# Diagonal blocks of step 1 on two engines, and the low part of step 0 behind the diagonal of its high part

## The chip, the cores and the metric

The kernel runs on one core of a Trainium2 chip. The metric is device time in microseconds (us); the profile comes from one execution of the program, recorded by the hardware profiler. The core's engines are TensorE (PE, matmuls; PEld is its weight load), VectorE (DVE), ScalarE (ACT), GpSimd (POOL) and SyncE (SP), which issues most of the DMAs. Each engine runs its own instructions in the order in which they were written into the program, and waits on semaphores for the others.

## The reference

Three layers follow each other: a delta-rule attention, a two-matrix feed-forward layer, and a soft mixture of eight experts whose gate weights are balanced by row and column normalisation.

```python
B, H, S, D = 4, 8, 768, 48
k_n = k / (norm(k) + 1e-6)
for t in range(S):                                 # delta rule, state (B, H, D, D)
    y[:, :, t] = q_t @ state
    state = state + b_t * outer(k_t, v_t - state^T k_t)
x = y as (B*S, H*D) = (3072, 384)
x = leaky(x @ w_in, 0.01) @ w_out                  # 384 -> 2048 -> 384
P = exp(x @ w_gate - max), then 8 times: rows to sum 1, columns to sum N/E
out = sum over 8 experts e of P[:, e] * (relu(x @ w1[e]) @ w2[e])    # 384 -> 1024 -> 384
```

## The kernel before, in words

The sequence of 768 tokens is cut into six steps `t` of 128 tokens, and the attention is computed by blocks. For each step and each of the four batches `b` (all eight heads at once) `part1` normalises the keys, transposes them (`kT`), forms the Gram products and keeps, as `a`, the strictly upper part scaled by beta. `a` is split into two float16 tensors: `nh`, its high part, and `nl`, the rest `a - nh`. `nh` also gets ones on its diagonal (a select on GpSimd). The 32x32 blocks on the diagonal of `a` are copied into `a_d`, four copies for each batch, and `solve(t)` inverts all of them at once on VectorE, column by column (`ld`, `tm`, `xs`), ending with a transpose into `xt`. `part2(t, b)` copies the inverses into `u` (four copies), transposes `u` into `x`, and grows the inverse from blocks of 16 or 32 to 128 by products of `x` with `nh` and of `u` with `p1`, whose results ScalarE copies back. Then come the products with the values; `nh` and `nl` are both read in one of them (`r_ps`). The first two steps (`SMALL`) start from blocks of 16.

The helper `spread` makes the copies into `a_d` and `u`: on ScalarE, except that of step 0 every second one goes to VectorE.

The feed-forward layer of a step (`main_a(t)`) runs beside the attention of the next one. The weights `wa` come as 64-bit floats and are converted on the way: `convert` reads each third of a chunk (`raw`), makes `cva`, `cvs` and `cvp` on ScalarE, VectorE and GpSimd, and writes it to a scratch tensor. This starts behind step 0's inverse.

Nothing of this is issued directly. `Recorder` notes every operation with its engine, a cost and its dependencies, and a planner places them (`place`, `tails`, `order`). Each operation starts with a rank: the length of the work that depends on it, a bias (`AHEAD` for attention, `EARLY` for the maxima of the expert weights) and a random jolt drawn with `SEED`. In ten rounds (`ROUNDS`) the planner places the work forwards, compares the planned end with the best so far, and replaces the ranks by the distance from the end in a backwards placement. The ranks of the best round are used. `emit` then issues everything in planned order (line 560 in the profile) and fills planned gaps of TensorE with matmuls on constants (line 1205, and `stir`). The order of the last step's feed-forward layer and of the expert stage (from about 735 us on) is planned elsewhere, by the class `Plan`.

The list `late` holds the `nl` subtractions. Those of step 0 (`late[0:B]`) get an added dependency, kept by a real wait: they may not start before the second transpose of `u` into `x` (`turned[1]`). The select that writes the diagonal of `nh` comes after the subtraction that reads `nh`.

The lines that matter are the constants (line 50 and those around it), `spread` (line 672), `halves` and the lines behind it in `part1` (from line 766), and the use of `late` further down.

Of the kernel before, what the change touches and what calls it, by code (L numbers as in the profile page):

```python
# [15 lines left out]
ACTF = mybir.ActivationFunctionType  # L16
ALU = mybir.AluOpType
# [3 lines left out]
B, H, S, D = 4, 8, 768, 48  # L21
C = 128
# [24 lines left out]
SMALL = (0, 1)  # L47

STIR = (145, 20)
AHEAD, EARLY = 50.0, 60.0  # L50
ROUNDS, SEED = 10, 7
NEAR = 0.02
FILL = 0.5
SLACK = 4.0
# [512 lines left out]
def delta_moe_kernel(ctx: ExitStack, tc: tile.TileContext, k_l, v_l, q_l, beta_l, wa_in, wg, wc, out):  # L567
# [5 lines left out]
    pe, act, dve, pool, sp = (rec.engine(*x) for x in zip(("PE", "ACT", "DVE", "POOL", "SP"), engines))  # L573
# [49 lines left out]
    for i in range(RING):  # L623
# [3 lines left out]
            nh=ring_p.tile([128, H, C], F16, name=f"nh{i}"),  # L627
            nl=ring_p.tile([128, H, C], F16, name=f"nl{i}"),
# [38 lines left out]
    def bank(name):  # L667
        return free.tile(range(6 if early else 3))

    late, grams = [], []  # L670

    def spread(t, blk, out, src):
        if t == 0 and blk % 2:
            dve.tensor_copy(out=out, in_=src)
        else:
            act.activation(out=out, in_=src, func=ACTF.Copy)
# [5 lines left out]
    def load_k(t):  # L682
        kraw[t] = a1_p.tile([128, B, H, D], F32, tag="kraw", name="kraw")
        if t == 0:
            for b in range(B):
                sp.dma_start(out=kraw[t][:, b], in_=k_l[t, :, b])
        else:
            sp.dma_start(out=kraw[t], in_=k_l[t])
# [27 lines left out]
    def part1(t):  # L716
        kr = kraw.pop(t)
        n2 = a1_p.tile([128, B, H], F32, tag="n2", name="n2")
        sn = a1_p.tile([128, B, H], F32, tag="sn", name="sn")
        rn = a1_p.tile([128, B, H], F32, tag="rn", name="rn")  # L720
        for bs in ([slice(b, b + 1) for b in range(B)] if t == 0 else [slice(0, B)]):
            for b in range(bs.start, bs.stop):
                sq = ring[(t * B + b) % RING]["kn"][:, :, 0:D]
                act.activation(out=sq, in_=kr[:, b], func=ACTF.Square)
                dve.tensor_reduce(out=n2[:, b], in_=sq, axis=AX.X, op=ALU.add)
            n, s0, r = n2[:, bs], sn[:, bs], rn[:, bs]
            dve.tensor_scalar(out=n, in0=n, scalar1=2.0 ** -110, scalar2=None, op0=ALU.max)
            act.activation(out=s0, in_=n, func=ACTF.Sqrt)
            dve.reciprocal(out=r, in_=s0)
            dve.tensor_tensor(out=r, in0=r, in1=n, op=ALU.mult)  # L730
            dve.tensor_tensor(out=r, in0=r, in1=s0, op=ALU.add)
            dve.tensor_scalar(out=r, in0=r, scalar1=0.5, scalar2=1e-6, op0=ALU.mult, op1=ALU.add)
            dve.reciprocal(out=r, in_=r)

        def normalise(b):
            r = ring[(t * B + b) % RING]
            dve.tensor_tensor(out=r["kn"][:, :, 0:D], in0=kr[:, b],
                              in1=rn[:, b].unsqueeze(2).to_broadcast([128, H, D]), op=ALU.mult)
        yield
        for b in range(B):  # L740
            normalise(b)
            if b == B - 1 and t + 1 < NT:
                load_k(t + 1)
            r = ring[(t * B + b) % RING]
            kn, kT, nh, nl = r["kn"], r["kT"], r["nh"], r["nl"]
            ps = bank("kt_ps")
            for p in range(NP):
                pe.transpose(out=ps[:, p * C:(p + 1) * C],
                             in_=kn[:, 2 * p:2 * p + 2].rearrange("p a d -> p (a d)"), identity=ident)
            act.activation(out=kT, in_=ps, func=ACTF.Copy)  # L750
            yield
            a = (at_p if t == 0 and b > 1 else a1_p).tile([128, H, C], F32, tag="uc" if t == 0 and b > 1 else "a32", bufs=2)
            gps = [bank("g_ps").rearrange("p (h c) -> p h c", h=4) for _ in range(2)]
            for j in range(4):
                for g in range(2):
                    kk = kT[64 * g:64 * g + D, j, :]
                    pe.matmul(out=gps[g][:, j], lhsT=kk, rhs=kk, start=True, stop=True)
            for g in range(2):
                for j in range(4):
                    h = 2 * j + g  # L760
                    g1 = dve.scalar_tensor_tensor(out=a[:, h], in0=gps[g][:, j], scalar=beta[:, t, b, h:h + 1], in1=upper,
                                             op0=ALU.mult, op1=ALU.mult)
                    grams.append(g1)
                yield

            def halves():
                act.activation(out=nh, in_=a, func=ACTF.Copy)
                late.append(pool.tensor_tensor(out=nl, in0=a, in1=nh, op=ALU.subtract))

            if t:  # L770
                halves()
            for blk in range(4):
                o = 32 * blk
                spread(t, blk, a_d[o:o + 32, :, b * H:(b + 1) * H], a[o:o + 32, :, o:o + 32].rearrange("p h j -> p j h"))
            if not t:
                halves()
            pool.affine_select(out=nh, in_=nh, pattern=[[0, H], [-1, C]], compare_op=ALU.not_equal,
                               fill=1.0, base=0, channel_multiplier=1)
            yield

    xt_of = {}
# [32 lines left out]
    def part2(t, b):  # L814
# [21 lines left out]
        for blk in range(4):  # L836
            o = 32 * blk
            spread(t, blk, u[o:o + 32, :, o:o + 32], xt[o:o + 32, :, b * H:(b + 1) * H].rearrange("p j h -> p h j"))
# [272 lines left out]
    if True:  # L1111
# [22 lines left out]

        setup2()
        run(part1(0))
        setup3()
        act.activation(out=wg_r, in_=wg_f, func=ACTF.Copy)
        dve.tensor_tensor(out=wg_r[:, :, E:2 * E], in0=wg_f[:, :, 0:E], in1=fr(wg_r[:, :, 0:E]), op=ALU.subtract)
        run(solve(0))  # L1140
        run(part1(1))
        attention(0, 0)
        attention(0, 1)
# [25 lines left out]
        for t in range(NT - 1):  # L1169
            rec.bias = 0.0  # L1170
            for n, _ in enumerate(main_a(t)):
                rec.flush()
                if t and n % 3 == 0:
                    rec.after = rec.steps[-1]
                    rec.bias = EARLY
                    next(mx_gen, None)
                    rec.after, rec.slack, rec.bias = None, 0.0, 0.0
            rec.bias = AHEAD
            if t + 2 < NT:
                run(part1(t + 2))  # L1180
            for b in range(B):
                attention(t + 1, b)
            if t + 2 < NT:
                run(solve(t + 2))
# [23 lines left out]
        pe, act, dve, pool, sp = engines  # L1208
# [200 lines left out]
        for i in range(NF1):  # L1409
# [6 lines left out]
            if i in tasks:  # L1416
                n, t = tasks[i]
# [12 lines left out]
        for c in range(KD):  # L1430
# [11 lines left out]
            out=cmax[:, 2 * E + t5:2 * E + t5 + 1], in_=xmax[:, t5], axis=AX.X, op=ALU.max))],  # L1442
# [277 lines left out]
        for u, (e, p) in enumerate(units):  # L1720
# [18 lines left out]
            x = [Pair(e, p, i) for i in range(4)]  # L1739
# [93 lines left out]
```

## Time and profile before

| | us |
|---|---|
| median of 3 runs | 2193.38 |
| lowest and highest run | 2190.36, 2196.22 |
| profiled execution, its own time | 2193.52 |
| its span, first to last instruction | 2191.7 |
| TensorE busy | 2100.6 (96%) |
| VectorE busy | 1674.5 (76%) |
| ScalarE busy | 1399.2 (64%) |
| GpSimd busy | 605.7 (28%) |

The page also cuts the span into 40 equal slices of about 55 us. TensorE's busy share, in tenths, is 6 7 8 8 9 8 in the first six slices, 9 (90% or more) in nearly all the others. All attention work carries the line number 560, that of the planner's issue, so groups are told apart by the names of their tiles. A row of a timeline begins with start and duration; "x4" means that four instructions in a row were merged, and the duration is that of all of them. Brackets at the end tell how long the engine was idle before, and what released it.

### The profile page before, as it was taken

Reading aid. Unit: us, or ns where it says so; the run is one execution under the profiler, and the core shown is the slowest. Engines: PE = TensorE matmul, PEld = TensorE weight load, DVE = VectorE, ACT = ScalarE, POOL = GpSimd, SP = SyncE. Lnnn points to the kernel's source line nnn. Section 1 sums busy time; section 2 is a strip of 40 time slices with the busy share of each in tenths; the row PEclk is TensorE's granted clock in tenths of the full one; section 3 lists DMA queues with packets and bytes.
Section 4 is the critical chain, followed back from the end, with each engine's and each line's share of the span. In section 5 each row is a group of like instructions: output and inputs, shape, how many; then the busy total and the mean of one; then the engine's idle time right before and its main releaser. Section 6 shows DMA issues by size and latency. Waiting matters only on the chain.

```text
span 2191.7 us, 43420 instructions
## 1 busy us (share of the span) xinstructions
PE 2100.6 (96%) x17219; PEld 1577.7 (72%) x17219; DVE 1674.5 (76%) x3313; ACT 1399.2 (64%) x2621; POOL 605.7 (28%) x672
## 2 busy tenths in 40 slices
PE   6788989999999999999999999999999999999999
PEld 5676767887877766766677777777777777777776
DVE  8676777649685567886777877877877877877877
ACT  5978746654756467768666656656656656656554
POOL 3654621111120161335215115115114114213100
PEclk8899989999999999999999999999999999999999
DMA  3566655755565652343223223333333333333321
GB/s 99 162 200 200 217 181 172 237 195 198 183 213 193 217 204 99 107 152 130 102 95 127 102 105 138 116 109 138 116 109 137 116 109 137 116 107 117 110 95 52
DMA packets 123452, 312.89 MB, mean 143 GB/s; under 512 B 14960, under 2 KB 66800, under 8 KB 117104
## 3 DMA queue, kind: packets, MB, share of 16 engines
q1 hardware_dynamic: 121088, 306.18, 40.8%
q10 hardware_dynamic: 2160, 3.93, 0.5%
q8 instruction: 135, 2.21, 0.4%
q14 instruction: 69, 0.57, 0.1%
HBM read 247.84 MB, written 62.13 MB: 141 GB/s over the span
## 4 chain that ended last, share of the span: by engine, by line
PE 77%; DVE 10%; ACT 7%; issue 3%; POOL 2%; DMA 1%; SPq 0%; DVEq 0%; ACTq 0%; POOLq 0%
PE b L1487 25%; PE b L1586 19%; PE ph L1586 11%; PE ph L1487 6%; PE bg L560 5%; PE po L560 5%; PE ph L560 4%; ACT u L560 2%; DVE tm L560 2%; DVE xs L560 1%; DVE a L560 1%; ACT p L560 1%; ACT cva L560 1%; DVE gl L560 1%; PE ph L1339 1%
## 5 line engine op out<-in xcount | busy, mean ns | idle before, releaser
L1248 POOL TENSOR_TENSOR stg<-stg 128x128 f32<-128x128 f32 (+2 forms) x248 | 166.6, 689 | 804.4 <-ACT stg L1245 800.3
L1487 PEld LDWEIGHTS <-w1h 128*128 128x128 f16 x2112 | 204.8, 98 | 221.0 <-issue 1.7
L1487 PE MATMUL b<-xoh,w1h 128*128 128x512 f16 x864 | 327.5, 379 | 0.0
L1487 PE MATMUL b<-xoh,w1l 128*128 128x512 f16 x864 | 327.5, 379 | 0.0
L1487 PE MATMUL b<-xol,w1h 128*128 128x512 f16 x864 | 327.4, 379 | 0.0
L1251 DVE SCALAR_TENSOR_TENSOR acc<-b,pm,acc 128x192 f32<-128x192 f32 (+1 forms) x357 | 155.4, 448 | 92.5 <-PE b L1586 91.6
L1487 PEld LDWEIGHTS <-w1l 128*128 128x128 f16 x1056 | 103.3, 98 | 124.6
L1245 ACT ACTIVATE b<-b 128x512 f32<-128x512 f32 x144 | 84.1, 584 | 139.3 <-PE b L1487 138.1
L1251 DVE SCALAR_TENSOR_TENSOR acc<-ph,pm,acc 128x192 f32<-128x192 f32 (+1 forms) x231 | 98.0, 432 | 76.9 <-PE ph L1586 76.8
L1245 ACT ACTIVATE c<-b 128x512 f32<-128x512 f32 x192 | 113.8, 593 | 63.0 <-PE b L1487 62.0
L560 PE MATMUL ph<-x1h,w 128*128 128x512 f32 (+1 forms) x504 | 143.5, 400 | 5.3 <-ACT leak L560 5.3
L1251 DVE SCALAR_TENSOR_TENSOR c<-c,c 128x512 f32<-128x512 f32 x192 | 134.7, 719 | 5.9 <-ACT c L1245 3.6
L1248 POOL TENSOR_TENSOR w2l<-stg,w2h 128x576 f16<-128x576 f32 (+1 forms) x96 | 108.6, 1150 | 107.0 <-ACT w2h L1245 107.0
L560 PE MATMUL po<-gh,w 128*128 128x512 f32 (+1 forms) x504 | 137.5, 397 | 0.6 <-ACT gh L560 0.6
L1248 DVE TENSOR_TENSOR c<-c,c 128x512 f32<-128x512 f32 x192 | 136.0, 712 | 2.5
L1251 DVE SCALAR_TENSOR_TENSOR c<-b,v 128x512 f32<-128x512 f32 x144 | 97.5, 689 | 43.9 <-PE b L1487 43.2
L560 DVE TENSOR_TENSOR gl<-leak,gh 128x512 fp32r<-128x512 f32 (+1 forms) x84 | 59.5, 708 | 76.7 <-ACT leak L560 65.7
L560 PEld LDWEIGHTS ph<-x1h,w 128*128 128x128 f32 x504 | 90.7, 194 | 22.9 <-ACT leak L560 5.7
L560 PEld LDWEIGHTS po<-gh,w 128*128 128x128 f32 x504 | 90.0, 192 | 18.4 <-ACT gh L560 2.1
L1248 POOL TENSOR_TENSOR w1l<-stg,w1h 128x384 f16<-128x384 f32 (+1 forms) x64 | 85.9, 1348 | 33.7 <-ACT w1h L1245 33.7
L1245 ACT ACTIVATE b<-ph 128x512 f32<-128x512 f32 x144 | 84.2, 585 | 6.6 <-PE ph L1487 2.5
L560 ACT ACTIVATE gh<-ph 128x512 fp32r<-128x512 f32 (+1 forms) x84 | 48.1, 572 | 50.9 <-PE ph L560 48.2
(510 smaller groups left out, 6653.4 us busy)
## 6 DMA issues: line engine op xcount, KB each, us to landing
w<-wa_scratch SPq DMA_DIRECT2D x100, 768.0 KB, 4.8
acc_scratch<-acc SPq DMA_DIRECT2D x84, 384.0 KB, 2.6
acc<-acc_scratch SPq DMA_DIRECT2D x84, 384.0 KB, 3.5
stg<-wc SPq DMA_DIRECT2D x64, 384.0 KB, 8.7
xoh<-xo_scratch SPq DMA_DIRECT2D x21, 1152.0 KB, 5.1
xol<-xo_scratch SPq DMA_DIRECT2D x21, 1152.0 KB, 8.0
raw<-wa SPq DMA_DIRECT2D x48, 256.0 KB, 2.9
wa_scratch<-cvp SPq DMA_DIRECT2D x48, 256.0 KB, 3.1
```

What stands on the lines that cost most here:

```text
L560: o.last = fn(*args, **{k: x.real() if isinstance(x, View) else x for k, x in kw.items()})
L1245: return vec("ACT", n, lambda e: e.activation(out=out, in_=src, func=func, scale=scale), reads, writes, **kw)
L1248: return vec(eng, n, lambda e: e.tensor_tensor(out=out, in0=a, in1=b, op=fn), reads, writes, **kw)
L1251: return vec("DVE", n, lambda e: e.scalar_tensor_tensor(out=out, in0=a, scalar=scalar, in1=b, op0=f0, op1=f1), reads, writes, **kw)
L1339: ordered(pe.matmul(out=self.ps, lhsT=wt[:, c * 128:(c + 1) * 128], rhs=xx[:, c], start=m == 0 and c == 0, stop=m == 2 and c == KD - 1))
L1487: ordered(pe.matmul(out=banks[b], lhsT=w[:, a], rhs=x[:, c].rearrange("p s k -> p (s k)"), start=start, stop=i == 2 and (a, c) == terms[-1 ...
L1586: ordered(pe.matmul(out=banks[b][:, 0:HD], lhsT=xx[:, o:o + 128], rhs=wt[:, t], start=first and k == 0 and j == 0, stop=k == NK - 1 and j ...
```

## The change

Three things are changed. `spread` gives every second copy to VectorE in step 1 as well as in step 0; this holds for the copies into `a_d` and for those into `u`. For step 0 the order around `nl` is another: `nh` is copied, gets its ones on the diagonal, then `nl = a - nh` is taken (its diagonal comes out as -1, as `a` is zero there), and a second select sets the diagonal of `nl` to zero. Only step 0's subtractions are put into `late` now, which makes no difference to its use. For the other steps the order stays. The planner's constants are `AHEAD` 30 in place of 50 and `SEED` 1 in place of 7.

```diff
--- before.py
+++ after.py
@@ -47,8 +47,8 @@
 SMALL = (0, 1)
 
 STIR = (145, 20)
-AHEAD, EARLY = 50.0, 60.0
-ROUNDS, SEED = 10, 7
+AHEAD, EARLY = 30.0, 60.0
+ROUNDS, SEED = 10, 1
 NEAR = 0.02
 FILL = 0.5
 SLACK = 4.0
@@ -670,7 +670,7 @@
     late, grams = [], []
 
     def spread(t, blk, out, src):
-        if t == 0 and blk % 2:
+        if t <= 1 and blk % 2:
             dve.tensor_copy(out=out, in_=src)
         else:
             act.activation(out=out, in_=src, func=ACTF.Copy)
@@ -763,19 +763,22 @@
                     grams.append(g1)
                 yield
 
-            def halves():
+            def diagonal(x, value):
+                return pool.affine_select(out=x, in_=x, pattern=[[0, H], [-1, C]], compare_op=ALU.not_equal,
+                                          fill=value, base=0, channel_multiplier=1)
+
+            if t:
                 act.activation(out=nh, in_=a, func=ACTF.Copy)
-                late.append(pool.tensor_tensor(out=nl, in0=a, in1=nh, op=ALU.subtract))
-
-            if t:
-                halves()
+                pool.tensor_tensor(out=nl, in0=a, in1=nh, op=ALU.subtract)
             for blk in range(4):
                 o = 32 * blk
                 spread(t, blk, a_d[o:o + 32, :, b * H:(b + 1) * H], a[o:o + 32, :, o:o + 32].rearrange("p h j -> p j h"))
             if not t:
-                halves()
-            pool.affine_select(out=nh, in_=nh, pattern=[[0, H], [-1, C]], compare_op=ALU.not_equal,
-                               fill=1.0, base=0, channel_multiplier=1)
+                act.activation(out=nh, in_=a, func=ACTF.Copy)
+            diagonal(nh, 1.0)
+            if not t:
+                late.append(pool.tensor_tensor(out=nl, in0=a, in1=nh, op=ALU.subtract))
+                diagonal(nl, 0.0)
             yield
 
     xt_of = {}
```

## Rows read from the trace of the kernel before

**Rows 1.** Busy us of each engine in stretches, their instructions, granted clock, DMA share, GB/s.

```profile
core 0: us, PE busy (x) PEld busy (x) DVE busy (x) ACT busy (x) POOL busy (x), PEclk, DMA share, GB/s
...
0.00:45.00 45.00, 36.18 (x289) 27.93 (x289) 39.68 (x141) 25.43 (x46) 12.53 (x26) 0.89 0.35 108
45.00:53.50 8.50, 0.03 (x1) 0.03 (x2) 8.50 (x24) 3.87 (x8) 6.08 (x4) 0.80 0.09 25
53.50:110.00 56.50, 43.33 (x511) 36.14 (x512) 37.89 (x87) 51.76 (x127) 35.65 (x38) 0.88 0.52 163
110.00:200.00 90.00, 75.62 (x739) 62.73 (x739) 62.62 (x170) 71.28 (x171) 47.13 (x57) 0.92 0.62 199
200.00:310.00 110.00, 91.98 (x746) 74.23 (x745) 82.08 (x197) 80.94 (x177) 55.88 (x57) 0.97 0.63 205
310.00:735.00 425.00, 412.26 (x3317) 337.21 (x3318) 287.78 (x651) 249.60 (x472) 62.18 (x65) 0.99 0.59 198
```

**Rows 2.** Waits, 40 to 110 us: engine, line, releaser, us in total, times, longest.

```profile
PE po L560 <- POOL nh L560: 8.6, 1, 8.6
```

**Rows 3.** Timeline of TensorE: last stir matmuls, first products with nh and nl.

```profile
42.95 1.92 PE L560 MATMUL ph<-stir 128*128 128x256 f16 x16
...
53.47 0.61 PE L560 MATMUL po<-x,nh 128*128 128x64 f16 x8 [8.60 <-POOL nh L560]
...
78.56 0.21 PE L560 MATMUL bg<-uc,nl 128*128 128x48 f16 x1
```

**Rows 4.** Timeline of VectorE, 30 to 77 us.

```profile
30.32 0.64 DVE L560 TENSOR_SCALAR n<-n 128x32 f32<-128x32 f32 x1
...
32.24 0.17 DVE L560 TENSOR_SCALAR rn<-rn 128x32 f32<-128x32 f32 x1
...
44.57 2.37 DVE L560 STREAM_TRANSPOSE x<-u 128x1024 f16<-128x1024 f16 x2
...
58.53 0.29 DVE L560 TENSOR_SCALAR cvs<-cva 128x256 f16<-128x256 f32 x1 [0.38 <-ACT cva L560]
...
74.77 1.88 DVE L560 TENSOR_SCALAR cvs<-cva 128x256 f16<-128x256 f32 x1 [4.32 <-ACT cva L560]
```

**Rows 5.** Timeline of ScalarE: step 0's last nh copy, and its idle time before 50.33.

```profile
29.77 1.04 ACT L560 ACTIVATE nh<-uc 128x1024 f16<-128x1024 f32 x1
...
50.33 1.31 ACT L560 ACTIVATE a_d<-a 32x256 f16<-32x256 f32 x2 [4.57 <-DVE a L560]
```

**Rows 6.** Timeline of GpSimd, 28 to 77 us.

```profile
28.50 2.44 POOL L560 TENSOR_SCALAR_AFFINE_SELECT mt<-mt 128x512 f32<-128x512 f32 x4 [3.35 <-ACT mt L560]
42.35 1.22 POOL L560 MEMSET xs<- 128x1056 f32 x2 [11.42 <-DVE tm L560]
45.90 4.25 POOL L560 TENSOR_TENSOR nl<-a,nh 128x1024 f16<-128x1024 f32 x2 [2.32 <-DVE x L560]
51.59 0.79 POOL L560 TENSOR_TENSOR cva<-cva,cvs 128x256 f32<-128x256 f32 x1 [1.44 <-DVE cva L560]
52.33 1.09 POOL L560 TENSOR_SCALAR_AFFINE_SELECT nh<-nh 128x1024 f16<-128x1024 f16 x1
...
72.28 4.22 POOL L560 TENSOR_TENSOR nl<-a,nh 128x1024 f16<-128x1024 f32 x2
```

**Rows 7.** Copies and selects by tile: ns min/median/max, first and last start us, forms.

```profile
L560 ACT ACTIVATE a_d<-a x16: 627/648/659, 50.3 to 90.5; 32x256 f16<-32x256 f32 x16
...
L560 ACT ACTIVATE u<-tm x16: 633/658/700, 141.5 to 200.1; 32x256 f16<-32x256 f32 x16
...
L560 DVE CAST u<-tm x8: 361/380/1146, 42.3 to 90.9; 32x256 f16<-32x256 f32 x8
...
L560 DVE CAST a_d<-uc x4: 370/375/379, 16.7 to 26.0; 32x256 f16<-32x256 f32 x4
L560 DVE CAST a_d<-a x4: 374/378/574, 19.4 to 26.4; 32x256 f16<-32x256 f32 x4
...
L560 POOL TENSOR_SCALAR_AFFINE_SELECT nh<-nh x24: 1086/1092/1527, 52.3 to 627.0; 128x1024 f16<-128x1024 f16 x24
```

**Rows 8.** The stretch with TensorE's most idle time after 320 us, columns as in rows 1.

```profile
540.00:560.00 20.00, 17.32 (x87) 14.08 (x87) 16.02 (x40) 10.93 (x20) 1.14 (x2) 0.91 0.54 188
```

## The prediction

> **What bounds the kernel now.** I read the windows by stage first [rows 1]. From 310 us on TensorE is busy for 412.3 of 425 us up to 735 us; the page's 40 slices show it nearly full from there to the end. Time can be won there only by removing matmuls, and the change removes none. Ahead of 310 us nothing is full: TensorE 0.03 of 8.5 us, then 43.3 of 56.5, 75.6 of 90 and 92.0 of 110, a part of that being filler matmuls on constants. ScalarE is the fullest engine right behind the gap: 51.8 of 56.5 us (92%) from 53.5 to 110, then 79% and 74%. VectorE has 67% and 70% from 53.5 to 200, but 39.7 of 45 us (88%) in the first stage, where the norms, the Gram products and step 0's inverse run on it one after the other.
>
> The second view is the list of waits, 40 to 110 us. Its one large wait of TensorE is 8.6 us for GpSimd's nh [rows 2]. The timelines say what it is. TensorE ends its stir matmuls at 44.87 and starts the first product with nh at 53.47 [rows 3]. VectorE delivers x for batches 0 and 1 in two transposes from 44.57 to 46.94 [rows 4], so that product lacks only nh. nh itself was copied early: the last of step 0's four copies starts at 29.77 [rows 5]. GpSimd then does, in its queue, the two nl subtractions (45.90, held behind the second transpose; 4.25 us), a weight product, and only then the diagonal of nh (52.33, 1.09 us) [rows 6]. The diagonal can't go first, because the subtraction must read nh before its diagonal is overwritten. So 7.6 us, from about 45.85 to 53.47, is waiting for an order that the values don't require. ScalarE has nothing to do for 4.57 us of it [rows 5].
>
> **The change part by part.** The profiled execution took 2193.52 us (span 2191.7), 0.1 us above the median of the three runs, so sums are made against 2193.5.
>
> Step 0's low part. nh gets its diagonal straight after its copy, and nl is taken afterwards, with a second select that clears its diagonal. No DMA is moved and no queue of SP. The first nh product no longer waits for the subtraction. Late next are x (45.8) and then ScalarE, which must copy each product out. What TensorE gains is at most the 7.6 us. What the path gains is what ScalarE can do ahead of time, as ScalarE is 92% busy behind the gap: its idle 4.57 us. Ends 0 and 7.6; I take 4.6, by that row.
>
> What this costs: the four selects of 1.09 us [rows 7] go from behind the transposes to somewhere between the copies and 45.8 us. There VectorE runs step 0's inverse. A TENSOR_SCALAR on VectorE at 30.32 took 0.64 us and ended with GpSimd's selects on mt (28.50 to 30.94), where its like at 32.24 took 0.17 [rows 4, 6]: GpSimd's selects can hold up VectorE. If all four stand in the way of the inverse the cost is 4 x 1.09 = 4.4 us, if they fit beside its transposes and reductions it is nothing. No row places them; I take half, 2.2.
>
> The four new selects on nl (4 x 1.09 = 4.4 us of GpSimd) come behind the subtractions. The first reader of nl is the product at 78.56 us [rows 3], while batch 0's and 1's nl were done at 50.15 [rows 6]: 28 us of room, and GpSimd is busy for 35.7 of 56.5 us there [rows 1]. I take nothing; without that cover it is 4.4 us. The subtractions are still held behind the second transpose; what queues behind them on GpSimd is weight conversion, as now.
>
> Step 1's copies. Eight of sixteen copies into a_d go from ScalarE (0.648 us) to VectorE, and eight of sixteen into u (0.658 us) [rows 7]. The first eight lie in the 92% stretch: 8 x 0.648 = 5.2 us. Ends 0 and 5.2; at 92% I take 4.8. The second eight lie from 141 to 200 us, where ScalarE is 79% busy and VectorE also has long chains: 8 x 0.658 = 5.3 us, ends 0 and 5.3; I take half, 2.6. VectorE takes 0.38 us for such a copy [rows 7], 16 x 0.38 = 6.1 us into stretches with about 19 and 27 us idle. I cost that at nothing, covered by that idle time; without it, 6.1 us.
>
> A copy on VectorE can also be held up by GpSimd. One of the copies to u took 1.146 us, in the stretch where GpSimd filled xs (42.35, 1.22 us); one of those to a_d took 0.574 [rows 6, 7]. Over the sixteen copies that VectorE has now that is (1.146 - 0.38) + (0.574 - 0.378), about 1 us. I take 1.0 for the new sixteen; the ends are 0 and 16 x 0.77 = 12.3.
>
> The same is seen on weight conversion: a TENSOR_SCALAR on cvs took 1.88 us while GpSimd subtracted (72.28 to 76.50), against 0.29 at 58.53 [rows 4, 6]. The Trainium skill speaks against the move here (SBUF — State Buffer, Who interferes with whom): VectorE's copies, casts and tensor_scalar may use a pair of ports that GpSimd uses too, and whichever of the two comes second is blocked until the other's instruction ends. By that rule each copy that meets GpSimd would be blocked, and the sum would be that of the third rival below; these rows agree in kind.
>
> The new order. SEED and AHEAD enter only the ranks from which the planner starts; the later of its ten passes replace them, and the pass that it thinks shortest is kept. So both edits draw another order for everything up to 735 us, of a like kind. Behind 735 us the order is written by another planner that the diff doesn't touch. I take 0. The ends: a gain can't exceed the 12.7 us that TensorE idles from 310 to 735 [rows 1]; for a loss the row is the worst 20 us of that stage, 540 to 560, with 2.7 us idle [rows 8]. One more such stretch in each of the four steps is 10.7 us.
>
> **The sum.** -4.6 + 2.2 - 4.8 - 2.6 + 1.0 = -8.8; 2193.5 - 8.8 = 2184.7 us. It carries to the end because TensorE is the bound from 310 us on: its work there starts that much earlier.
>
> **The rivals.**
> The gain is eaten ahead of 310 us (0.24). ScalarE is at 79% and 74% from 110 to 310, so other chains (weight conversion through three engines, step 2's inverse) may set the pace and take up whatever arrives early. Then the copies bring nothing, and of the first part 4.6 - 2.2 = 2.4 us is left: 2191.1. For it: no engine is full there [rows 1]. Against: ScalarE is the fullest up to 110 us, and nearly as full as TensorE with its fillers up to 200.
>
> The stall stays under another name (0.08). If the planner puts the diagonals late, or batch 0's product queues behind other work, the first part gives nothing: -4.8 - 2.6 + 1.0 = -6.4, 2187.1. That would be the change not doing what it says.
>
> The port takes it back (0.06). Every new copy meets GpSimd at the 0.77 us of the one above (12.3 us), and all four selects lie on the inverse (4.4): -4.6 - 4.8 - 2.6 + 4.4 + 12.3 = +4.7, 2198.2. It turns slower once copies and selects together cost over 12.0 us. Of the sixteen copies of now only two were held up, hence the small chance. It is the rule that the Trainium skill's page SBUF — State Buffer (Who interferes with whom) states, applied to every copy.
>
> The new order is worse (0.14). TensorE is at 97% from 310 to 735, so another draw has more to lose than to win. At four stretches like 540 to 560 (+10.7), and with the head's gain down to 3.6 us, it is +7.1: 2200.6. It turns slower once the new order loses more TensorE time from 310 on than the head gives. For it: the ranks are drawn anew. Against: it is made by the same planner, which keeps its best of ten.
>
> **How the numbers follow.** Forecast 0.48; the rivals 0.24, 0.08, 0.06, 0.14. A measurement here can tell about 0.3% from no change, 6.6 us: under 2186.8 is faster, over 2200.0 slower. Faster: most of the forecast (0.44), nearly half of the stall that stays (0.04), some of the eaten gain with a lucky order (0.05) and a little more, 0.55. Slower: the worse order and the port, and lower chances within the others, 0.18, counting that the order's loss may be well above its row. Same: 0.27. The low end takes the first part at its 7.6 us, all copies (10.5) and no costs, with 2 us from the order: 2193.5 - 20.1, about 2173. The high end reaches to the port's case and most of the worse order, 2199.
>
> **What would show it.** In the changed kernel: the wait of TensorE for GpSimd's nh gone and the first product on nh near 46 us; step 0's four selects on nh ahead of 46 us, and step 0's inverse no longer than before; eight casts more on VectorE to a_d and eight more to u, near 0.38 us each; ScalarE's busy time lower by about 10 us up to 200 us; the last filler matmuls and the stretch of full TensorE some 9 us earlier; idle TensorE time from there to the end of the attention stage near 12.7 us. The prediction is wrong if step 0's inverse is longer by over 4 us, if the full stretch doesn't start earlier, or if TensorE's idle time behind it grows by more than what was won.

## The result: slower, 2212.64 us

| | before | after |
|---|---|---|
| median, us | 2194.8 | 2212.64 |
| lowest and highest run, us | 2190.36, 2196.97 | 2210.28, 2214.42 |
| span of the profiled execution, us | 2191.7 | 2212.6 |
| TensorE busy in it, us | 2100.6 | 2113.0 |

The ratio of the times is 1.0086, with a 95% interval of 1.0072 to 1.0101: 16 to 22 us slower. The forecast was 2184.7 us, its range ended at 2199, and slower had a chance of 0.18. The forecast was wrong in sign.

The windows by stage of the changed kernel answer to [rows 1] (busy us and instructions of TensorE, its weight loads, VectorE, ScalarE, GpSimd; granted clock of TensorE, DMA share, GB/s). The granted clock has two levels in these traces, full speed (2.4 GHz) and half of it (1.2 GHz); the row gives the mean over the stretch, with full speed as 1:

```profile
0.00:45.00 45.00, 31.33 (x249) 24.19 (x250) 39.47 (x137) 23.45 (x42) 16.48 (x29) 0.92 0.33 108
45.00:53.50 8.50, 4.98 (x43) 3.57 (x43) 7.05 (x8) 6.44 (x20) 4.83 (x4) 0.61 0.00 1
53.50:110.00 56.50, 44.54 (x522) 38.15 (x521) 44.80 (x101) 43.60 (x105) 30.68 (x31) 0.83 0.43 133
110.00:200.00 90.00, 75.54 (x732) 65.52 (x732) 73.77 (x176) 67.75 (x162) 45.90 (x53) 0.88 0.54 163
200.00:310.00 110.00, 87.89 (x713) 69.13 (x713) 88.60 (x212) 74.01 (x173) 55.67 (x67) 0.94 0.64 204
310.00:735.00 425.00, 403.81 (x3118) 329.91 (x3118) 278.13 (x636) 244.20 (x456) 69.89 (x65) 0.99 0.61 202
```

And the first row of its page, the busy time of the whole span:

```profile
PE 2113.0 (95%) x17252; PEld 1589.4 (72%) x17252; DVE 1696.2 (77%) x3329; ACT 1389.4 (63%) x2605; POOL 612.3 (28%) x676
```

TensorE's busy time that still lies ahead at a given moment is the page's total less the windows up to there. At 735 us it was 2100.6 - 659.4 = 1441.2 us before and is 2113.0 - 648.1 = 1464.9 us now: the changed kernel is 23.7 us behind. At 310 us it was 1853.5 and is 1868.7: 15.2 us behind. So some 15 us are lost ahead of 310 us and another 8.5 from 310 to 735, where TensorE idles 425 - 403.8 = 21.2 us in place of 12.7; behind 735 us, 2.8 us less idling comes back. The stretch ahead of 310 has two losses in these rows, and a third in the filler matmuls. TensorE idles 3.0 us more from 53.5 us on, and its granted clock is 0.83, 0.88 and 0.94 where it was 0.88, 0.92 and 0.97 [rows 1]. The mean from 53.5 to 310 us is 0.89 against 0.93; 0.04 x 256.5 is about 10 us of full-speed time, some 8 of it while TensorE was busy (208.0 us there), by this estimate. The planner's fillers (line 1205, now 1208) took 38.2 instead of 34.4 us up to 310. The whole span agrees: of the 20.9 us that it grew, 8.5 are idle time and 12.4 busy time (2.9 of filler matmuls, the rest the same products for longer).

The timelines of the changed kernel (start, duration, engine, what; in brackets the idle time before and its releaser), which answer to [rows 3 to 6]:

```profile
48.02 0.58 PE L560 MATMUL bg<-x,nh 128*128 128x64 f16 x8 [5.54 <-DVE x L560]
```

```profile
44.39 2.30 DVE L560 CAST u<-tm 32x256 f16<-32x256 f32 x4
46.72 2.37 DVE L560 STREAM_TRANSPOSE x<-u 128x1024 f16<-128x1024 f16 x2
...
51.61 1.98 DVE L560 TENSOR_SCALAR cva<-cva 128x256 f32<-128x256 f32 x1 [0.15 <-ACT cva L560]
```

```profile
48.70 1.10 ACT L560 ACTIVATE p<-bg 32x128 f16<-32x128 f32 x4 [1.77 <-PE bg L560]
```

```profile
23.69 2.28 POOL L560 TENSOR_SCALAR_AFFINE_SELECT nh<-nh 128x1024 f16<-128x1024 f16 x2
...
29.02 2.13 POOL L560 TENSOR_SCALAR_AFFINE_SELECT nh<-nh 128x1024 f16<-128x1024 f16 x2 [0.21 <-ACT nh L560]
...
49.18 2.13 POOL L560 TENSOR_TENSOR nl<-uc,nh 128x1024 f16<-128x1024 f32 x1 [3.55 <-DVE x L560]
51.27 2.17 POOL L560 TENSOR_TENSOR nl<-a,nh 128x1024 f16<-128x1024 f32 x1
```

The order is the one that was meant. nh has its diagonal by 31.15 us, ahead of the transposes; nl is taken behind them; the first product with nh starts at 48.02 instead of 53.47 us [rows 3] and waits for x, not for GpSimd; ScalarE copies its result at 48.70, where the kernel before made its first such copy at 56.70:

```profile
56.70 0.27 ACT L560 ACTIVATE p<-po 32x128 f16<-32x128 f32 x1
```

By tile (ns min/median/max, first and last start), answering to [rows 7]:

```profile
L560 DVE CAST a_d<-a x12: 362/374/1277, 19.3 to 110.6; 32x256 f16<-32x256 f32 x12
```

```profile
L560 DVE CAST u<-tm x16: 362/380/1149, 44.4 to 201.6; 32x256 f16<-32x256 f32 x16
```

```profile
L560 POOL TENSOR_SCALAR_AFFINE_SELECT nl<-nl x4: 1090/1143/1274, 63.9 to 101.9; 128x1024 f16<-128x1024 f16 x4
```

The new casts and selects cost about what was expected in the median (0.374, 0.380 and 1.143 us). What is late is something else. SP's DMA issues of converted weights, first and last, in the kernel before and then in the changed one (in the changed one the first row holds two issues):

```profile
55.26 0.60 SPq L560 DMA_DIRECT2D wa_scratch<-cvp  x1
...
266.12 0.52 SPq L560 DMA_DIRECT2D wa_scratch<-cvp  x1
```

```profile
62.07 1.26 SPq L560 DMA_DIRECT2D wa_scratch<-cvp  x2
...
298.95 0.52 SPq L560 DMA_DIRECT2D wa_scratch<-cvp  x1
```

Conversion begins 6.8 us later and ends 32.8 us later. And of TensorE's waits from 53 to 310 us in the changed kernel (us in total, times, longest) the first, now the longest, is absent from the kernel before:

```profile
PE ph L560 <- DMA w<-wa_scratch: 8.7, 5, 4.2
PE bg L1208 <- ACT p L560: 5.9, 4, 2.7
PE po L560 <- DVE gl L560: 5.9, 5, 2.6
```

### The profile page after: what moved, and what is told of

The parts are those of the page before. It is cut to its first block, busy times and chain, and to the rows that moved or that the text cites. A ratio compares the mean times of both kernels' runs of the same rounds, so it can differ in the third digit from the quotient of the medians.

```text
span 2212.6 us, 43523 instructions
## 1 busy us (share of the span) xinstructions
PE 2113.0 (95%) x17252; PEld 1589.4 (72%) x17252; DVE 1696.2 (77%) x3329; ACT 1389.4 (63%) x2605; POOL 612.3 (28%) x676
## 4 chain that ended last, share of the span: by engine, by line
PE 75%; DVE 12%; ACT 7%; issue 3%; DMA 2%; POOL 2%; SPq 0%; ACTq 0%; DVEq 0%; POOLq 0%
PE b L1490 25%; PE b L1589 19%; PE ph L1589 10%; PE ph L1490 6%; PE bg L560 5%; PE po L560 4%; PE ph L560 4%; DVE tm L560 2%; DVE xs L560 2%; ACT u L560 1%; DVE cva L560 1%; ACT a_d L560 1%; DVE gl L560 1%; DMA w<-wa_scratch 1%; DVE stir L560 1%
## 5 line engine op out<-in xcount | busy, mean ns | idle before, releaser
L560 ACT ACTIVATE gh<-ph 128x512 fp32r<-128x512 f32 (+1 forms) x84 | 48.2, 574 | 83.1 <-PE ph L560 82.0
```

The lines of the kernel that those rows point to most:

```text
L560: o.last = fn(*args, **{k: x.real() if isinstance(x, View) else x for k, x in kw.items()})
```

## The experiments

Two kinds of kernels are told apart. Those whose label begins with f keep the old planned order, instruction by instruction, and only exchange or add the instructions in question. Those that begin with c, n or s let the planner order everything anew. Those that begin with a start from the changed kernel and keep its order. The table gives the time against runs of the kernel before on the same chip, the start of VectorE's casts of step 0's inverse into u, the start of the first product with nh, and the start of the last issue of converted weights (the last three in us from the start of the span).

| kernel | ratio, 95% interval | us against before | inverse done | first nh product | last converted |
|---|---|---|---|---|---|
| before | | | 42.3 | 53.5 | 266 |
| after | 1.0086 [1.0072, 1.0101] | +18.9 | 44.4 | 48.0 | 299 |
| f_copies | 1.0019 [1.0010, 1.0028] | +4.2 | 42.4 | 54.2 | 269 |
| f_order | 1.0015 [1.0005, 1.0025] | +3.3 | 44.6 | 48.6 | 270 |
| f_both | 1.0021 [1.0011, 1.0031] | +4.6 | 44.5 | 48.1 | 270 |
| f_extra | 1.0005 [0.9995, 1.0015] | +1.1 | 42.3 | 53.4 | 266 |
| c_const | 0.9989 [0.9977, 1.0001] | -2.4 | 41.6 | 48.5 | 277 |
| c_copies | 0.9990 [0.9980, 0.9999] | -2.2 | 42.8 | 53.9 | 269 |
| c_order | 1.0095 [1.0077, 1.0114] | +20.8 | 47.3 | 50.8 | 295 |
| c_order4 | 1.0075 [1.0058, 1.0092] | +16.5 | 46.5 | 50.0 | 287 |
| c_edits | 1.0052 [1.0034, 1.0070] | +11.4 | 47.9 | 51.5 | 284 |
| n_early | 1.0007 [0.9995, 1.0020] | +1.5 | 46.1 | 49.6 | 277 |
| n_late | 0.9971 [0.9958, 0.9985] | -6.4 | 41.9 | 46.6 | 262 |
| n_extra | 1.0110 [1.0094, 1.0126] | +24.1 | 43.5 | 54.7 | 294 |
| n_extra3 | 1.0034 [1.0021, 1.0047] | +7.5 | 44.5 | 51.5 | 287 |
| s_order | 1.0052 [1.0037, 1.0067] | +11.4 | 44.8 | 48.2 | 278 |
| s_before | 1.0029 [1.0021, 1.0038] | +6.4 | 41.3 | 48.2 | 275 |
| s_copies | 1.0058 [1.0044, 1.0071] | +12.7 | 42.2 | 49.2 | 272 |
| a_act | 1.0111 [1.0091, 1.0130] | +24.3 | 44.4 | 48.1 | 307 |
| a_free | 1.0065 [1.0050, 1.0080] | +14.3 | 44.4 | 48.0 | 292 |

### Each edit in the old order

f_copies issues step 1's sixteen copies on VectorE at the places that they had on ScalarE.

```diff
+        elif t == 1 and blk % 2:
+            rec.note("ACT", nc.vector.tensor_copy, "activation", (), dict(out=out, in_=src))
```

> The order of the kernel before is kept as it was; only step 1's sixteen copies (8 into a_d, 8 into u) are issued on VectorE in their old places. Theory P (GpSimd and VectorE hold each other up, and weight conversion pays): the copies cost VectorE more than 0.38 us each and ScalarE, which runs in its old order, wins little: 0 to +6 us against before. The prediction's sum: ScalarE was the fullest engine, so -4 to -8 us. Theory D (only the new draw of the order is to blame): -2 to -8 us, since the edit itself is then a gain.

+4.2 us. ScalarE's busy time from 53.5 to 110 us falls from 51.76 [rows 1] to 46.06 us, and no time is won; the granted clock of that stretch is 0.77.

```profile
53.50:110.00 56.50, 45.77 (x484) 38.20 (x485) 40.81 (x97) 46.06 (x116) 36.77 (x39) 0.77 0.53 166
```

f_order moves step 0's selects on nh right behind the copies of nh, and puts the selects on nl in the places that they leave.

```diff
-                act.activation(out=nh, in_=a, func=ACTF.Copy)
+                o = act.activation(out=nh, in_=a, func=ACTF.Copy)
+                if not t:
+                    o.calls.append((nc.gpsimd.affine_select, (), diagonal(nh, 1.0)))
...
+            if not t:
+                o.calls[:] = [(nc.gpsimd.affine_select, (), diagonal(nl, 0.0))]
```

> The order of the kernel before is kept; only step 0's four selects on nh are issued right behind the copies of nh, and the four selects on nl take their old places. The prediction's sum: the first product with nh 6 to 7 us earlier and the end 2 to 5 us earlier. Theory C (the wait for nh never was on the chain that sets the end, since ScalarE in its own order only reaches the copies of that product at 56.7 us): the first product some 6 us earlier and the end within 2 us of before. Theory P: VectorE's inverse of step 0 up to 4 us longer, the end 0 to +4 us.

+3.3 us, though the wait for nh is gone. In f_order, TensorE's longest wait from 40 to 110 us, then the timelines of TensorE, ScalarE and VectorE:

```profile
PE bg L560 <- ACT p L560: 10.7, 1, 10.7
```

```profile
48.64 0.40 PE L560 MATMUL po<-x,nh 128*128 128x64 f16 x8
...
61.46 0.59 PE L560 MATMUL bg<-u,p 128*128 128x64 f16 x8 [10.68 <-ACT p L560]
```

```profile
52.59 1.31 ACT L560 ACTIVATE a_d<-a 32x256 f16<-32x256 f32 x2 [4.57 <-DVE a L560]
...
58.95 0.27 ACT L560 ACTIVATE p<-po 32x128 f16<-32x128 f32 x1
```

```profile
44.57 2.22 DVE L560 CAST u<-tm 32x256 f16<-32x256 f32 x4
```

The first product with nh starts at 48.64 us, and the product that takes up its result (through ScalarE's copy p) at 61.46, behind a wait of 10.68 us for that copy. ScalarE copies p at 58.95, because in its queue p stands behind the copies into a_d and nh of step 1, and these wait for VectorE's a. Its idle time ahead of them is 4.57 us, as it was [rows 5], only 2.26 us later, by as much as the inverse is later (44.57 against 42.33).

f_both joins the two edits in the old order.

```diff
+        elif t == 1 and blk % 2:
...
+                    o.calls.append((nc.gpsimd.affine_select, (), diagonal(nh, 1.0)))
```

> Both edits in the old order of the kernel before. The sum of the two runs above: the prediction's sum says -6 to -11 us, theory P 0 to +8 us, theory D -4 to -11 us. If it isn't slower than before by over 6 us, most of the 18 us that the change lost comes from the new order and not from what the edits cost by themselves.

+4.6 us; the wait is again one for p (11.2 us). In the old order the two edits of the work together cost a quarter of what the change cost when planned anew.

### The constants and each edit, planned anew

c_const takes only the constants:

```diff
-AHEAD, EARLY = 50.0, 60.0
-ROUNDS, SEED = 10, 7
+AHEAD, EARLY = 30.0, 60.0
+ROUNDS, SEED = 10, 1
```

> The kernel before with AHEAD 30 and SEED 1 and none of the other edits, planned anew. Theory D: most of the loss is here, +10 to +20 us. Theory P: the operations are those of before, so within 6 us of before, and weight conversion ends near 266 us as before, not near 298.

-2.4 us: with unchanged work, the new start of the planner (this one draw) isn't what costs 19 us.

c_copies, c_order and c_edits keep AHEAD 50 and SEED 7 and take the copies (the first of these two edits), the order of step 0's low part (the second, as in the change), or both.

```diff
-        if t == 0 and blk % 2:
+        if t <= 1 and blk % 2:
```

```diff
+            diagonal(nh, 1.0)
+            if not t:
+                late.append(pool.tensor_tensor(out=nl, in0=a, in1=nh, op=ALU.subtract))
+                diagonal(nl, 0.0)
```

> Step 1's copies alone, planned anew with AHEAD 50 and SEED 7. In the old order they cost +4 us. Theory R (the planner has to place more work on the pair VectorE and GpSimd, finds a longer order, and the loss is both): +3 to +8 us against before. Theory D (chance of one draw): anything between -6 and +8, not tied to when weight conversion ends.

> Step 0's low part alone, planned anew with AHEAD 50 and SEED 7. In the old order it cost +3 us. Theory R: the four selects on nh ahead of the inverse and the four on nl are the larger part of what the planner must place on the pair, so most of the loss is here: +8 to +15 us, and weight conversion ends well behind 266 us. The prediction's sum for this part: -2.4 us.

> Both edits, with the constants of before (AHEAD 50, SEED 7). Theory R: slower than before whatever the start, +6 to +14 us, a few us better than the changed kernel. Theory D: back near before, -6 to +3 us, since the draw alone was bad.

Copies -2.2, order +20.8, both +11.4 us. In these plans the loss comes with the edit of step 0's low part.

a_act keeps the changed kernel's order and gives step 1's copies back to ScalarE.

```diff
+            o = dve.tensor_copy(out=out, in_=src)
+            if t:
+                o.calls[:] = [(nc.scalar.activation, (), dict(out=out, in_=src, func=ACTF.Copy))]
```

> The changed kernel in its own order, with step 1's sixteen copies issued on ScalarE in their places. Theory P (the copies hold up weight conversion on VectorE and GpSimd): 4 to 10 us faster than the changed kernel, +8 to +14 us against before. If the order itself is the loss: within 4 us of the changed kernel, +14 to +22 us against before.

+24.3 against +18.9 us: in that order the copies on VectorE save some 5 us (the two numbers are known to within some 4 and 3 us). What they do depends on the order around them: they cost 4.2 us in the old order, go with a gain of 2.2 in a new plan, and save about 5 in the changed kernel's.

### Which part of the new order

n_early is c_order without the selects on nl (its diagonal keeps its -1: the step is left out); n_late also holds the selects on nh behind the second transpose, as the kernel before has them in effect. n_extra is the kernel before with the added selects on nl and nothing moved. The edits in this order, n_late's on top of n_early's:

```diff
-                diagonal(nl, 0.0)
```

```diff
+        for o, x in zip(ones_of[0:B], (turned[1], turned[1], turned[1], turned[1])):
+            o.deps.add(x)
+            o.held.add(x)
```

```diff
+            if not t:
+                pool.affine_select(out=nl, in_=nl, pattern=[[0, H], [-1, C]], compare_op=ALU.not_equal,
+                                   fill=0.0, base=0, channel_multiplier=1)
```

> Step 0's low part in the new order, but without the four selects that clear the diagonal of nl (left out, so nl keeps -1 there), planned anew with AHEAD 50 and SEED 7. If the four selects on nh ahead of step 0's inverse are the loss: +10 to +18 us, nearly that of the part with both (+20), the inverse some 2 to 5 us longer. If the four added selects are the loss: -2 to +4 us.

> As the run above (nl's diagonal not cleared, left out), but the four selects on nh of step 0 also wait for the second transpose of u into x, where the subtractions start. Only the sequence of select and subtraction differs from the kernel before. If the place ahead of the inverse is the loss: back at before, -4 to +3 us, the first copy of the inverse on VectorE near 42.3 us and the last converted weight near 266 us. If the flipped sequence itself loses (attention gets ready earlier and takes the engines from weight conversion): +6 us and more.

> The kernel before with four further selects on nl of step 0 behind those on nh (they write zeros where nl is zero already), planned anew with AHEAD 50 and SEED 7. If GpSimd's time in this stage is paid for in full, since VectorE is held up by it and weight conversion runs through both: 4.4 us of selects cost +3 to +8 us. If GpSimd has room there, as the prediction said: -3 to +3 us.

Step 0's inverse and first product with nh, in n_early:

```profile
46.09 2.19 DVE L560 CAST u<-tm 32x256 f16<-32x256 f32 x4
```

```profile
49.60 0.59 PE L560 MATMUL po<-x,nh 128*128 128x64 f16 x8 [5.33 <-DVE x L560]
```

and in n_late:

```profile
41.91 2.20 DVE L560 CAST u<-tm 32x256 f16<-32x256 f32 x4
```

```profile
46.60 0.61 PE L560 MATMUL po<-x,nh 128*128 128x64 f16 x8 [6.22 <-POOL nh L560]
```

n_early is within the noise of before (+1.5), n_late is faster (-6.4), though TensorE waits 6.22 us for nh in it. With the selects on nh beside it the inverse ends at 46.1 us, with the selects held behind it at 41.9. n_extra differs from the kernel before by four selects that change no value, and loses 24.1 us: the added selects, not the order of nh, go with the loss.

### The selects themselves, or the plan around them

f_extra adds the same four selects in the old order; n_extra3 repeats n_extra with SEED 3, c_order4 repeats c_order with SEED 4; s_order is c_order with SEED 3 and without one rule of the planner's model, by which a select on GpSimd may not run at the same time as a VectorE copy, TENSOR_SCALAR or instruction on two inputs from SBUF (for the other GpSimd operations the rule stays). The edits of f_extra and of s_order:

```diff
+            if not t:
+                o.calls.append((nc.gpsimd.affine_select, (), dict(
+                    out=nl, in_=nl, pattern=[[0, H], [-1, C]], compare_op=ALU.not_equal,
+                    fill=0.0, base=0, channel_multiplier=1)))
```

```diff
-            return lat - 0.03, lat, True
+            return lat - 0.03, lat, method != "affine_select"
```

> The kernel before in its old planned order, with one harmless select on nl issued right behind each of step 0's four selects on nh (4 x 1.09 us more on GpSimd, nothing else moved, no planning anew). Theory A (the selects cost so much only because the planner writes another order around them): 0 to +4.4 us over before, about 2195, and the last write of converted weights within 3 us of before's 266. Theory B (the selects themselves hold up the chain of weight conversion and VectorE on the chip): +12 us or more, over 2205, last write from 280 on.

> The same added selects on nl as in n_extra, planned anew from another random draw (SEED 3 in place of 7, AHEAD 50). Theory A1 (n_extra's 24 us are one bad draw): within 8 us of before, under 2201. Theory A2 (the selects push the planner to a later weight conversion whatever the draw): 2205 or more, last write of converted weights from 285 on.

> The new order of step 0's low part alone, as in c_order, planned from another draw (SEED 4 in place of 7, AHEAD 50). Theory A1 (draw): under 2201. Theory A2 (whatever the draw): 2205 or more, last write of converted weights from 285 on.

> The new order of step 0's low part alone, but the planner doesn't reserve VectorE and GpSimd against each other for a select (for subtractions and products it still does); AHEAD 50, SEED 3. Theory A3 (the reservation is what delays the conversion): last write of converted weights under 275 and the time at or under before's, 2185 to 2195. Theory A2 with real blocking on the chip: VectorE's instructions beside the selects get longer instead, and the time stays at 2203 or more.

Two of f_extra's selects on GpSimd's timeline, each on nl right behind its one on nh, and its window from 53.5 to 310 us:

```profile
52.30 1.08 POOL L560 TENSOR_SCALAR_AFFINE_SELECT nh<-nh 128x1024 f16<-128x1024 f16 x1
53.35 1.08 POOL L560 TENSOR_SCALAR_AFFINE_SELECT nl<-nl 128x1024 f16<-128x1024 f16 x1
```

```profile
53.50:310.00 256.50, 214.66 (x1993) 176.98 (x1993) 183.32 (x451) 203.79 (x473) 142.15 (x156) 0.91 0.60 193
```

The same window of the kernel before, of n_extra, and of the changed kernel:

```profile
53.50:310.00 256.50, 210.93 (x1993) 173.09 (x1993) 182.59 (x451) 203.97 (x474) 138.66 (x152) 0.93 0.60 194
```

```profile
53.50:310.00 256.50, 210.37 (x1884) 169.38 (x1884) 182.84 (x436) 200.35 (x463) 143.34 (x158) 0.87 0.54 174
```

```profile
53.50:310.00 256.50, 207.97 (x1963) 172.80 (x1962) 207.17 (x487) 185.37 (x438) 132.25 (x150) 0.89 0.56 174
```

In the old order the four selects cost 1.1 us (interval -1.1 to +3.3), with 142.15 against 138.66 us of GpSimd and the other engines' busy time hardly changed but TensorE's, whose clock is 0.91. With the same work planned anew, TensorE gets a clock of 0.87 and executes 1884 instead of 1993 matmuls, fillers among them, from 53.5 to 310 us. So the selects cost next to nothing where the order is kept, and 24.1 and 7.5 us in the two orders that the planner wrote around them.

s_before and s_copies take the same planner's rule away with no added select, from SEED 1 and, with step 1's copies on VectorE, from SEED 2. Both have s_order's edit above; s_copies also has this one:

```diff
-        if t == 0 and blk % 2:
+        if t <= 1 and blk % 2:
```

> The kernel before planned anew without reserving VectorE and GpSimd against each other for a select (subtractions and products still reserve); AHEAD 50, SEED 1. If the reservation costs real time: under 2188, TensorE further ahead at 310 us. If the chip blocks the pair just as the reservation assumed: 2190 to 2200, with longer VectorE instructions beside the selects. If a plan from another draw is all there is to it: anything within 6 us of before's 2193.

> Step 1's copies shared with VectorE, step 0's low part as before, and no reservation for selects in the plan; AHEAD 50, SEED 2. Copies worth 2 us as in c_copies and the reservation real: 2183 to 2188, faster than both kernels. If only the draw counts: 2188 to 2200, like c_copies' 2191.1 or worse.

+6.4 and +12.7 us. Without the rule, all three plans are slower than the kernel before, with the added selects (s_order, +11.4) and without: taking the rule away doesn't take the loss away. Each of the three has a draw of its own, so how much of their loss is the missing rule isn't shown.

### The wait for converted weights

a_free keeps the changed kernel's order, but step 0's feed-forward layer loads one and the same chunk each time, which is ready early.

```diff
+        if items_a[i][0] == 0:
+            o.calls[0][2]["in_"] = wa[0]
```

> The changed kernel in its own order, but in step 0 each load of converted weights takes the first chunk again, so that TensorE waits for the conversion of one chunk alone (left out: step 0 multiplies by the weights of its own chunks). If weight conversion is what paces the stage to 310 us in the changed kernel: 8 to 16 us faster than it, +2 to +10 us against before, TensorE's waits for w gone. If conversion is beside the path: within 3 us of the changed kernel.

+14.3 against +18.9 us. The two intervals (11 to 18 and 16 to 22 us) overlap, so the gain of some 5 us is hardly clear of the noise. TensorE's wait for weights falls from 8.7 to 5.5 us and doesn't vanish:

```profile
PE ph L560 <- DMA w<-wa_scratch: 5.5, 3, 3.2
```

The edit doesn't take conversion off the path. SP issues its DMAs in the written order, and the loads of w still stand behind loads and writes of the conversion, which wait for VectorE and GpSimd. In a_free, SP's longest wait in total from 225 to 262 us, and its issues ahead of the longest of TensorE's three waits:

```profile
SPq L560 <- DVE cva L560: 18.8, 8, 4.9
```

```profile
253.32 1.19 SPq L560 DMA_DIRECT2D wa_scratch<-cvp  x2
256.24 0.33 SPq L560 DMA_DIRECT2D raw<-wa  x1
256.62 0.42 SPq L560 DMA_DIRECT2D w<-wa_scratch  x1
```

So a late conversion is probably a part of the loss; how large a part stays open. It isn't all that can go wrong: s_copies has conversion done at 272 us, c_const at 277, and the first loses 12.7 us where the second loses nothing.

## Why the prediction was wrong

**The step that failed is the term of the new order: "So both edits draw another order for everything up to 735 us, of a like kind", taken at 0.** The forecast was 8.8 us faster. f_both, with the edits in the old order, is 4.6 us slower, and the changed kernel 18.9: some 13 us of the error lie in the terms for the edits themselves, and some 14 us in the order. c_const shows that the constants alone, in this draw, are harmless, as the step said. But the work had changed as well. With the planner's rule in force, six plans have the added selects (after, c_order, c_order4, c_edits, n_extra, n_extra3), and all six are slower, by 7.5 to 24.1 us. The four new plans without them (c_const, c_copies, n_early, n_late) lie between -6.4 and +1.5. The selects' own time is not it (f_extra). The rival "the new order is worse", at a chance of 0.14, named the right place, the order, but blamed the fresh draw of the ranks, which does no harm in c_const. It was also priced in the wrong stretch: by TensorE's idle time from 310 us on, at most 10.7 us (8.5 measured), while some 15 us are lost ahead of 310 us, where the rows showed no full engine and a granted clock of 0.88 to 0.97.

**"I take nothing" for the four selects on nl: right in the old order, wrong in the plan.** The 28 us of room belonged to the order of before. In the changed kernel the selects run from 63.9 us on, and the first product with nl comes at 66.85 us in place of 78.56 [rows 3]. TensorE's list of waits has none for nl there; the price shows only in the plan.

**"What the path gains is what ScalarE can do ahead of time": wrong, -4.6 us taken, none found.** The wait went, as forecast. But ScalarE's idle time of 4.57 us had VectorE's a as its releaser [rows 5], not a product of TensorE; f_order shows it unchanged, and TensorE waits for p instead. The row that was taken as the size of the gain named another cause in its brackets. In the changed kernel, where the planner moved ScalarE's work too, p is copied 8.0 us earlier (48.70 against 56.70), and TensorE is behind at 310 us all the same. The table has the same in another form: the first nh product starts anywhere from 46.6 to 54.7 us, and the time doesn't follow it (48.0 us with +18.9, 53.4 with +1.1).

**The cost of the selects beside the inverse: right in size, partly by luck.** 2.2 us were taken as half of an upper end, with no row that placed the selects. The inverse ended 2.06 us later in the changed kernel and 2.24 in f_order, but 5.0 and 5.6 us later in the plans of c_order and c_edits, above the upper end of 4.4.

**The copies: -4.8 and -2.6 us taken, +4.2 us in the old order and -2.2 planned anew.** The durations were right (0.374 and 0.380 us). What the sixteen new copies lost to GpSimd was 2.1 us in the changed kernel and 1.1 in f_copies (the sum of their times above 0.376 us each), where 1.0 was taken: the third rival, in which every copy meets GpSimd for 12.3 us in all, didn't come. ScalarE's busy time up to 200 us fell by 11.1 us (152.3 to 141.2), as forecast. That ScalarE was 92% busy didn't make it the bound: f_copies frees 5.7 us of it and gains nothing. That the copies bring nothing was the first rival, and f_order, where the wait turned up under the name of ScalarE's p, is the second.

**"The stretch of full TensorE some 9 us earlier": wrong.** TensorE is 15.2 us behind at 310 us, and idles 21.2 us from there to 735 us where 12.7 were expected. Two of the three signs of being wrong came true, this stretch and the idle time behind it; the third, an inverse longer by over 4 us, didn't.

What stays open is why the planner writes a worse order around the selects. The rows show what the worse orders have in common (a mean clock of 0.87 to 0.92 from 53.5 to 310 us, where the plans without the selects have 0.92 to 0.96; weights converted by 284 to 299 us, where those have 262 to 277), not which decision begins it. Neither sign is enough: the three plans without the rule have a clock of 0.93 to 0.95 and are done by 272 to 278 us, and still lose 6.4 to 12.7 us, two of them with no added select. That four more selects need a worse order isn't shown either: six plans were tried, no more, and the ends that the planner itself foresaw for its plans weren't compared. Of the kernels with all of the computation only c_copies has an interval below that of no change, and by a hair: 0.9990 [0.9980, 0.9999]. An order like that of n_late, with nl's diagonal cleared without GpSimd, wasn't tried.

## What to carry to other kernels

Where a program writes the order, time an edit twice, in the old order and planned anew: here the selects cost 1.1 us in the one and 7.5 to 24.1 in the other, and a plan can cost more than any instruction in it. Before you count an idle time as a gain, read its releaser: an engine that waits for something other than what you speed up gains nothing there. An engine that is 92% busy need not be the bound: here 5.7 us less work on it won no time.

## Hardware that was not expected

VectorE's TENSOR_SCALAR can be held up across two instructions of GpSimd; two rows here look like it. In the changed kernel, VectorE's timeline, GpSimd's, and the like instructions by tile:

```profile
280.41 3.17 DVE L560 TENSOR_SCALAR cva<-raw 128x256 int32<-128x256 int32 x1
```

```profile
280.38 2.13 POOL L560 TENSOR_TENSOR nl<-a,nh 128x1024 f16<-128x1024 f32 x1
282.44 0.98 POOL L560 MEMSET xs<- 128x1056 f32 x1
```

```profile
L560 DVE TENSOR_SCALAR cva<-raw x16: 280/290/3165, 53.5 to 280.4; 128x256 int32<-128x256 int32 x16
```

It takes 0.29 us in the median; this one began 0.03 us after GpSimd's subtraction, and ended at 283.58 us, 0.16 us behind the end of the memset that came after it. In c_const the same shows on a like instruction, with VectorE's row first and then GpSimd's:

```profile
77.86 3.02 DVE L560 TENSOR_SCALAR cvs<-cva 128x256 f16<-128x256 f32 x1
```

```profile
77.71 2.13 POOL L560 TENSOR_TENSOR nl<-a,nh 128x1024 f16<-128x1024 f32 x1
79.78 0.95 POOL L560 MEMSET u<- 128x1024 f16 x1
```

The profile counts such time as VectorE being busy. So the higher busy time of VectorE in the changed kernel (207.17 against 182.59 us from 53.5 to 310 us) is in part waiting: by an estimate from the trace, each instruction's time above the median of its like, this part grew from 27 to 40 us. The Trainium skill (SBUF — State Buffer, Who interferes with whom) says that whichever of the two has the shared pair keeps it for its whole instruction. The rows agree that VectorE waits (3.17 us in place of 0.29), and suggest beyond it that GpSimd's next instruction can go ahead of VectorE's waiting one (spans on GpSimd are rough in the profile, but 3.17 and 3.02 us are longer than the subtraction of 2.13 alone). In the timeline above, a TENSOR_SCALAR of 1.98 us at 51.61 lies beside the subtraction at 51.27 alone.
